# Chunked attention with memory, then a gated feed-forward layer: loads and clears in another order, attention paced per block, six tiles' values computed by tokens, one batch's memory rows copied later

## The chip, the core and the metric

The kernel runs on one core of a Trainium2 chip. The core has a matrix engine (TensorE, "PE" in the profile; its weight loads are "PEld"), VectorE ("DVE"), ScalarE ("ACT"), GpSimd ("POOL") and SyncE ("SP"). Each engine works through its own instructions strictly in the order in which the program puts them, and waits at an instruction until what it needs is there. GpSimd and SyncE also issue DMA transfers. Matrix products go into PSUM, from which VectorE or ScalarE copy them to SBUF. The metric is the device time of one execution in microseconds (us).

## The reference

Four batches, 8 heads, 768 tokens, head size 64. Queries go in chunks of 32; each chunk sees 8 memory keys and the 56 keys from 16 before it to 8 after it. The attention output, heads side by side (3072 x 512), goes through a gated layer.

```python
for c in range(nc):                                  # chunks of 32
    k_full = np.concatenate([mem_k, k[:, :, l_start:r_end]], axis=2)
    v_full = np.concatenate([mem_v, v[:, :, l_start:r_end]], axis=2)
    scores = scale * np.matmul(q_c, k_full.transpose(0, 1, 3, 2))
    a = np.exp(scores - np.max(scores, axis=-1, keepdims=True))
    a = a / (np.sum(a, axis=-1, keepdims=True) + 1e-09)
    out[:, :, c_start:c_end] = np.matmul(a, v_full)
x = out.transpose(0, 2, 1, 3).reshape(B * S, H * D)  # 3072 x 512
gate = np.maximum(x @ w_gate, 0.0)                   # 512 x 1536
val = x @ w_val
result = gate * val @ w_out                          # 1536 x 512
```

## The kernel before

The 3072 tokens are 24 tiles of 128, six to a batch; tile a has four chunks. Tiles are gathered into seven blocks of 3, 3, 4, 4, 4, 4 and 2 tiles (`BLOCKS`), the units of the feed-forward layer.

**Attention of one tile a.** The names are those of the planner's operations, with the line of the work. `t(a,1)` and `t(a,0)` turn keys and queries around: for tiles 0 to 13 on TensorE, for two tiles at once (L221, a "pair": K3 is the load of the keys of tiles 6 and 7), for later ones by a DMA transpose on SP (L261; the keys of tile 14 still on TensorE, L252). `tc` copies them to kT and qT. `s(a)` are the scores (L287, 32 small products), `max`, `sub`, `sum`, `rec`, `nrm` the softmax on VectorE (L300, L307, L319, L323, L330), `exp` on ScalarE (L315). `p(a)` turns the probabilities around: on TensorE up to tile 13 (L336, copied by `pc`), by a DMA transpose from tile 14 on (L340). `v(a)` multiplies them by the values (L353): the stationary operand is a 128 x 128 piece of `v_bd`, in which two heads' memory and context rows stand on the diagonal, and 32 columns of probabilities stream through it, 16 products to a tile. The result has features on the partitions; `x(a)` copies it to `xT`, one buffer to a block, two buffers in all.

**v_bd.** There are two sets, used by batches in turn. Set 0 is filled for batch 0 by four spread copies of a pattern (L171, VectorE), set 1 is cleared by four memsets on GpSimd (L128, "z0" to "z3"). Into them go the values by DMA (L179) and the memory rows, for batches 1 to 3 by eight copies on VectorE each, `mr(b, ...)` (L159). v(6) to v(11) need all of `mr(1, ...)`.

**Feed-forward.** `f(block, m, 0)` and `f(block, m, 1)` are the products with w_gate and w_val for the m-th 128 of the 1536 columns (L378, four matmuls each), then `relu` on ScalarE (L384), `gate` on VectorE (L390). `o(block, tile, ...)` is the product with w_out (L399), copied out by ScalarE (L88) and stored by SP (L409). Blocks 0 and 1 run interleaved, by quarters of the weights (w0 to w3), since the weights arrive in four groups of four DMAs; the later blocks run one after the other.

**Order.** The program is written out by a planner, `schedule()`, which goes through a list of operations with assumed durations, due times and priorities, and gives every engine its order. At run time only the order remains, with the semaphores between engines. Loads go on GpSimd in the order of the string `LOADS`; each DMA of GpSimd waits for the eighth before it to land. `pace(a)` says which first-layer product must have been started before the attention work of tile a may be: `LEAD[block]` products ahead of an even spread. `MEM_LEAD[b]` says how many tiles ahead of batch b's first scores its memory rows may be copied. Early on, where TensorE would sit idle, the plan puts in idle products of 128 x 128 (L370), whose results nobody reads.

Of the kernel before, what the change touches and what calls it, by code (L numbers as in the profile page):

```python
# [20 lines left out]
def kernel(  # L21
# [12 lines left out]
    nc = tc.nc  # L34
# [15 lines left out]
    CTX = 16 + CH + 8  # L50
    NSET = 2
    BLOCKS = [3, 3, 4, 4, 4, 4, 2]
    LEAD = [0, 0, 0, 4, 4, 4, 4, 4]
    LAST = ((0, 384), (384, 512))
    BY_DMA = (14, 15)
    BY_DMA_P = 14
    LANDING = 3.0
    PAIRS = 7
    MEM_BY_SP = 0
    MEM_LEAD = (0, 4, 4, 4)  # L60
    BESIDE = 13.0
    LOADS = """K0 Q0 i K1 Q1 v00 v01 K2 v02 v03 Q2 w0 v10 v11 v12 v13 w1 z0 w2 z1
               K3 z2 w3 z3 m Q3 K4 o0 o1 Q4 K5 b1 Q5 K6 Q6 k14 q14 k15 q15 k16 b2 q16 k17
               q17 k18 q18 k19 q19 k20 q20 k21 q21 k22 b3 q22 k23 q23"""

    KEY_RUNS = ((CH, KW, 0), (0, CH, NMEM), (KW, 64, KW))
    assert sum(BLOCKS) == NT and NMEM == 8 and D == 64 and H == 8

    const = ctx.enter_context(tc.tile_pool(name="const", bufs=1))
    ldpool = ctx.enter_context(tc.tile_pool(name="ldpool", bufs=15))  # L70
    ktpool = ctx.enter_context(tc.tile_pool(name="ktpool", bufs=6))
    prpool = ctx.enter_context(tc.tile_pool(name="prpool", bufs=6))
    kvpool = ctx.enter_context(tc.tile_pool(name="kvpool", bufs=2))
    smpool = ctx.enter_context(tc.tile_pool(name="smpool", bufs=2))
    xtpool = ctx.enter_context(tc.tile_pool(name="xtpool", bufs=2))
    gvpool = ctx.enter_context(tc.tile_pool(name="gvpool", bufs=2))
    grpool = ctx.enter_context(tc.tile_pool(name="grpool", bufs=3))
    opool = ctx.enter_context(tc.tile_pool(name="opool", bufs=3))
# [7 lines left out]
    def copy(eng, o, i):  # L86
        if eng is nc.scalar:
            nc.scalar.copy(o, i)  # L88
        else:
            eng.tensor_copy(o, i)  # L90
# [124 lines left out]
    def pair_t(r, i):  # L215
        ps = TMP["pair", r, i] = aps.tile([128, 2, HP, 128], BF16, tag="aps", name="qk_ps")
        x = qk_b.pop(("pair", r, i))
        for j in range(2):
            for hp in range(HP):
                for r in range(2):  # L220
                    nc.tensor.transpose(ps[D * r:D * r + D, j, hp, :], x[:, 2 * hp + r, j, :], ident_b)  # L221
# [124 lines left out]
    def values(a):  # L346
# [3 lines left out]
        for hp in range(HP):  # L350
            for g in range(4):
                r = slice(CH * g, CH * g + CH)
                nc.tensor.matmul(ps[:, hp, r], lhsT=v_bd[b % NSET][:, hp, 4 * t + g, :],  # L353
                                 rhs=x[:, hp, r], start=True, stop=True)

    def x_copy(a, eng):
        blk = block_of[a]
        j = a - starts[blk]
        if j == 0:
            xTs[blk] = xtpool.tile([128, NFC, 128 * BLOCKS[blk]], F16, name="xT")  # L360
        copy(eng, xTs[blk][:, :, 128 * j:128 * j + 128], TMP.pop(("x", a)))
# [45 lines left out]
    def store(blk, t, cols):  # L407
# [8 lines left out]

    ops, loads = {}, []
    room = {"aps": 2, "sps": 1, "fps": 4, "mx": 2, "dif": 2, "p": 2, "sm": 2, "rinv": 2, "pn": 2, "pT": 6,
            "qk": 15, "xT": 2, "gv": 2, "gr": 3, "o": 3, "kv": 2, "pr": 6, "kt": 6}

    def op(key, eng, fn, deps=(), prio=(0,), take=(), give=(), after=()):
        ops[key] = dict(eng=eng, fn=fn, deps=list(deps), prio=prio, take=list(take), give=list(give),
                        after=list(after))
# [4 lines left out]
    def psum(n):  # L428
        return {"ACT": 0.21 + 0.83e-3 * n, "DVE": 0.22 + 1.04e-3 * n}
# [34 lines left out]
    for a in range(NT):  # L464
        b, t = divmod(a, TPB)
        last = t == TPB - 1
        for i in (1, 0):
            if a < 2 * PAIRS:
                if a % 2:
                    continue  # L470
                op(("t", a, i), {"PE": 0.48}, lambda e, a=a, i=i: pair_t(a // 2, i), [("qk2", a // 2, i), "ib", ("new", b)],
                   (1, a - i, 0), ["aps"], ["pr"], pace(max(a - i, 0)))
                if i:
                    for j in range(2):
                        op(("tc", a + j, i), psum(HP * 128), lambda e, a=a, j=j: pair_k_copy(a // 2, j, engine[e]),
                           [("tc", a, i) if j else ("t", a, i)], (1, a - i, j), (), ["aps"] * j)
# [30 lines left out]
        else:  # L507
# [1 line left out]
            op(("pc", a), {"PE": 0.01}, lambda e: None, [("p", a)], (1, a, 9))  # L509
        blk = block_of[a]  # L510
        j = a - starts[blk]
        op(("v", a), {"PE": 0.45}, lambda e, a=a: values(a),
           [("pc", a)] + [("vl", b, 0 if b else t // 3, n) for n in range(2 if b else 2 * HP)]
           + ([("mr", b, par, hp) for par in range(2) for hp in range(HP)] if b else []), (1, a, 10), ["aps"] + (["xT"] if j == 0 else []), ["pT"],
           [("v", a - 1)] if a else [])
        op(("x", a), psum(HP * 128), lambda e, a=a: x_copy(a, engine[e]), [("v", a)], (1, a, 11), (), ["aps"],
           [("x", a - 1)] if a else [])


    n_early = sum(x < TPB for x in starts)  # L520
# [60 lines left out]
        load(("z", hp), 0, 1.5, lambda: zero(nc.gpsimd, v_bd[1], hp))  # L581

    def load_batch(b):
        deps = [("z", HP - 1)] if b < NSET else [("v", TPB * (b - NSET + 1) - 1)]
        for par in range(2):
            for hp in range(HP):
                if b <= MEM_BY_SP:
                    op(("mr", b, par, hp), {"SP": 0.73}, lambda e, b=b, par=par, hp=hp: mem_rows(b, par, hp, nc.sync),
                       deps + [(("vm", par), 0.2)], (0, par, hp))
                else:  # L590
                    op(("mr", b, par, hp), {"DVE": 0.6}, lambda e, b=b, par=par, hp=hp: mem_rows(b, par, hp, nc.vector),
                       deps + [("vm", par)], (1.5,), (), (), [("s", TPB * b - MEM_LEAD[b])])
        for par in range(2):
            load_v_op(b, 0, par, 0, HP * NCH, par, [], deps)
# [26 lines left out]
    def timed(d):  # L621
        return isinstance(d, tuple) and len(d) == 2 and isinstance(d[1], float)

    MOVE = {"t": 1.3, "p": 1.3, "mr": 0.7}

    def schedule():
        done, started, times = {}, set(), [0.7]
# [28 lines left out]
        while len(started) < len(ops) + len(loads):  # L656
# [8 lines left out]
            while moved:  # L665
                moved = False
                for e in ("POOL", "PE", "ACT", "DVE", "SP"):
# [18 lines left out]
                    else:  # L686
# [15 lines left out]
                        d = o["eng"][e] * (1.8 if e == "PE" and t < 24.0 and key[0] in ("t", "p") else 1.0)  # L702
                        end = t + d
                        done[key] = end + (0.25 if e == "PE" else 0.08)
                        if e == "SP" and key[0] in "tp":
# [55 lines left out]
```

## Time and profile before

| | us |
|---|---|
| median of 3 runs (lowest, highest) | 245.66 (244.87, 248.21) |
| the profiled execution, of which the page tells | 247.63 |
| its span, first to last instruction | 245.9 |
| first feed-forward product starts | 27.53 |
| first w_out product starts | 70.76 |
| VectorE, ScalarE, GpSimd busy | 151.1, 110.6, 76.8 |

The page's slices divide the span in 40 equal parts of 6.1 us. DMAs keep busy up to about 130 us, when the last queries have landed:

```profile
DMA  7999999999999999999994232530112211012102
```

Groups of instructions are told by line, engine and tile, with the number of instructions, busy time, mean duration of one, and the idle time just before them with what ended it. A matmul's own duration includes the fill of the array; what it costs in a row of matmuls is the distance from start to start. In time lines the columns are start, busy time, engine, line, what is done, and in brackets the idle time before. In lists of waits they are the total, the number, and the longest.

### The profile page before, as it was taken

The numbers are of one execution on the slowest core, as the hardware profiler recorded it, in microseconds if no ns is written. First come the engines' busy times: TensorE is split into PE (matmuls) and PEld (weight loads), VectorE is DVE, ScalarE is ACT, GpSimd is POOL, SyncE is SP. The second block draws the span as 40 slices with busy tenths as digits, with TensorE's granted clock in tenths as the row PEclk, the third lists the DMA queues.
The fourth block names the chain that finished last, engine by engine and source line by source line (L and its number), as shares of the span: only waits on it lengthen the run. The fifth ranks groups of instructions, "written<-read, shape, count | busy, mean of one in ns | idle before, by whom it ended". The sixth has DMA issues, their size and how long they took to land.

```text
span 245.9 us, 6041 instructions
## 1 busy us (share of the span) xinstructions
PE 231.0 (94%) x2528; PEld 127.9 (52%) x2528; DVE 151.1 (61%) x270; ACT 110.6 (45%) x232; POOL 76.8 (31%) x88
## 2 busy tenths in 40 slices
PE   0969989969999999999999999999999999999994
PEld 0858656545654644544544444544444444444872
DVE  2886785596889867778937776427871166310430
ACT  2546744434664447645424653235452234312432
POOL 7799999952445554418000000000000000000000
PEclk9997999997999999999999999999999999999999
DMA  7999999999999999999994232530112211012102
GB/s 78 130 125 175 158 198 179 154 199 167 139 138 181 198 174 202 147 151 122 146 195 123 44 67 43 156 104 3 21 24 64 89 43 21 0 40 91 43 4 85
DMA packets 111612, 27.18 MB, mean 111 GB/s; under 512 B 102752, under 2 KB 108640, under 8 KB 111584
## 3 DMA queue, kind: packets, MB, share of 16 engines
q0 software_dynamic: 91840, 16.61, 92.3%
q1 hardware_dynamic: 19744, 10.18, 18.1%
q8 instruction: 20, 0.33, 0.5%
q14 instruction: 8, 0.07, 0.1%
HBM read 33.24 MB, written 6.29 MB: 161 GB/s over the span
## 4 chain that ended last, share of the span: by engine, by line
PE 76%; POOL 10%; DMA 7%; DVE 3%; issue 2%; SPq 1%; ACT 0%; DVEq 0%
PE out_ps L399 26%; PE v_ps L378 22%; PE g_ps L378 22%; POOL v_bd L179 3%; PE xT_ps L353 3%; DMA w_val_sb<-in_moe_w_val_dram 3%; DMA vmem<-in_mem_v_dram 3%; POOL v_bd L128 2%; POOL w_gate_sb L114 2%; PE s_ps L287 2%; POOL w_val_sb L114 2%; DVE v_bd L159 2%; DMA vmem_f<-in_mem_v_dram 1%; PE qk_ps L221 1%; POOL qk_p L210 1%
## 5 line engine op out<-in xcount | busy, mean ns | idle before, releaser
L390 DVE TENSOR_TENSOR gvT<-v_ps,g_relu 128x512 f16<-128x512 f32 (+2 forms) x84 | 51.4, 612 | 55.2 <-PE v_ps L378 42.5
L378 PE MATMUL v_ps<-xT,w_val_sb 128*128 128x512 f16 (+2 forms) x336 | 77.1, 353 | 0.7 <-DMA w_val_sb<-in_moe_w_val_dram 0.7
L378 PE MATMUL g_ps<-xT,w_gate_sb 128*128 128x512 f16 (+2 forms) x336 | 76.7, 352 | 0.3 <-DMA w_gate_sb<-in_moe_w_gate_dram 0.3
L384 ACT ACTIVATE g_relu<-g_ps 128x512 f16<-128x512 f32 (+2 forms) x84 | 44.9, 535 | 55.0 <-PE g_ps L378 49.4
L399 PE MATMUL out_ps<-w_out_sb,gvT 128*128 128x512 f16 (+2 forms) x300 | 65.3, 371 | 0.0
L378 PEld LDWEIGHTS <-w_val_sb 128*128 128x128 f16 x336 | 31.8, 99 | 28.0 <-issue 2.0
L378 PEld LDWEIGHTS <-w_gate_sb 128*128 128x128 f16 x336 | 31.7, 98 | 27.2 <-issue 1.1
L399 PEld LDWEIGHTS <-gvT 128*128 128x128 f16 x300 | 27.9, 98 | 30.4
L179 POOL DMA_DIRECT2D v_bd<-in_v_dram x24 | 27.7, 1165 | 13.1 <-issue 9.1
L88 ACT COPY o_sb<-out_ps 128x512 f32<-128x512 f32 (+2 forms) x25 | 14.2, 566 | 37.6 <-PE out_ps L399 37.5
L315 ACT ACTIVATE p_exp<-dif 128x64 f16<-128x64 f32 (+2 forms) x72 | 19.5, 336 | 9.6 <-DVE dif L307 9.6
L159 DVE COPY v_bd<-vmem 8x1536 f16<-8x1536 f16 x24 | 18.7, 798 | 1.2 <-DMA vmem<-in_mem_v_dram 1.0
L300 DVE TENSOR_REDUCE mx<-s_ps 128x8 f32<-128x512 f32 x24 | 16.6, 690 | 3.5 <-PE s_ps L287 3.1
L319 DVE TENSOR_REDUCE sm<-p_exp 128x8 f32<-128x512 f16 x24 | 16.3, 677 | 3.5 <-ACT p_exp L315 3.1
L330 DVE TENSOR_TENSOR p_n<-p_exp,rinv 128x512 f16<-128x512 f16 x24 | 16.4, 685 | 0.3
L307 DVE TENSOR_TENSOR dif<-s_ps,mx 128x512 f32<-128x512 f32 x24 | 16.4, 682 | 0.2
L353 PEld LDWEIGHTS <-v_bd 128*128 128x128 f16 x384 | 12.7, 96 | 4.7 <-issue 0.3
L88 ACT CAST xT<-xT_ps 128x512 f16<-128x512 f32 x17 | 9.9, 585 | 8.8 <-PE xT_ps L353 8.8
L201 POOL DMA_DIRECT2D qk_b<-in_k_dram x10 | 8.9, 887 | 15.6 <-issue 8.8
L353 PE MATMUL xT_ps<-pT,v_bd 128*128 128x32 f16 x384 | 13.2, 176 | 0.0
L221 PE MATMUL qk_ps<-ident_b,qk_p 128*64 128x128 bf16 x224 | 10.6, 248 | 2.3 <-DMA qk_p<-in_k_dram 2.3
L88 ACT COPY kT<-qk_ps 128x512 bf16<-128x512 bf16 x10 | 7.1, 742 | 12.3 <-PE qk_ps L221 6.3
(46 smaller groups left out, 136.5 us busy)
## 6 DMA issues: line engine op xcount, KB each, us to landing
out_dram<-o_sb SPq DMA_DIRECT2D x23, 256.0 KB, 2.4
v_bd<-in_v_dram POOLq DMA_DIRECT2D x5, 672.0 KB, 16.0
qk_p<-in_k_dram POOLq DMA_DIRECT2D x7, 256.0 KB, 5.7
qk_p<-in_q_dram POOLq DMA_DIRECT2D x7, 256.0 KB, 6.5
w_gate_sb<-in_moe_w_gate_dram POOLq DMA_DIRECT2D x8, 192.0 KB, 5.4
w_val_sb<-in_moe_w_val_dram POOLq DMA_DIRECT2D x8, 192.0 KB, 6.3
w_out_sb<-in_moe_w_out_dram POOLq DMA_DIRECT2D x2, 768.0 KB, 11.4
qk_b<-in_k_dram POOLq DMA_DIRECT2D x10, 128.0 KB, 12.9
```

The lines of the kernel that those rows point to most:

```text
L88: nc.scalar.copy(o, i)
L159: eng.tensor_copy(o, i)
L179: nc.gpsimd.dma_start(dst[64 * par + NMEM + s0:64 * par + NMEM + s1, c0:c1, D * par:D * par + D], bass.AP(tensor=v.tensor, offset=v[b, HP ...
L300: nc.vector.reduce_max(SM[a, "mx"], s4, axis=AX.X)
L307: nc.vector.tensor_tensor(out=SM[a, "dif"].rearrange("p (m r) a s -> p r m a s", r=2), in0=S_ps.pop(a).rearrange("p r (m a) s -> p r m a s ...
L315: nc.scalar.activation(p[:, :, :, s0:s0 + k1 - k0], dif[:, :, :, k0:k1], ACT.Exp, scale=SCALE)
L330: nc.vector.tensor_tensor(out=P_n[a], in0=SM.pop((a, "p")), in1=rinv_b, op=ALU.mult)
L353: nc.tensor.matmul(ps[:, hp, r], lhsT=v_bd[b % NSET][:, hp, 4 * t + g, :], rhs=x[:, hp, r], start=True, stop=True)
L378: nc.tensor.matmul(ps, lhsT=w[:, f, 128 * m:128 * m + 128], rhs=xTs[blk][:, f, :], start=(f == 0), stop=(f == NFC - 1))
L384: nc.scalar.activation(st["r", m], st.pop((0, m)), ACT.Relu)
L390: nc.vector.tensor_tensor(out=st["gv"][:, m, :], in0=st.pop((1, m)), in1=st.pop(("r", m)), op=ALU.mult)
L399: nc.tensor.matmul(st["o", t, cols], lhsT=st["gv"][:, m, 128 * t:128 * t + 128], rhs=w_out_sb[:, m, slice(*cols)], start=(m == 0), stop=(m ...
```

## The change

- `LOADS` is permuted: all pair loads of tiles 0 to 5 and two of the clears stand ahead of the first half of batch 0's values; weight groups w0, w1 and w2 stand ahead of the second half; w3 follows; two clears (z0, z3) and w_out come later, and the single loads of tiles 14 to 23 are no longer in the order of the tiles.
- `LEAD` differs from block to block, so attention is put at other places between the feed-forward products.
- `MEM_LEAD` of batch 1 goes from 4 to 0: its memory rows are copied after the scores of tile 6 in the plan (in the order that results, after those of tile 9) rather than of tile 2.
- For tiles 18 to 23 (`BY_DMA_X`), the values are computed with the probabilities as the stationary operand, 128 rows by 32 columns, and 128 columns of `v_bd` streaming: the result has tokens on the partitions. `xn_copy` brings it to a new buffer and a DMA transpose on SP puts it into `xT`.
- `ldpool` has 14 buffers, not 15, `ktpool` 5, not 6, and there is a new pool of 2 for the copied values.
- Some assumed durations and dependences of the planner differ: a pair's transpose 0.57 for 0.48, a copy of memory rows 0.8 for 0.6, and loads of batch 1 depend on all four clears.

The number of TensorE products in the feed-forward layer, of scores, and of bytes loaded is unchanged. There are 111 idle products, where there were 119.

```diff
-    LEAD = [0, 0, 0, 4, 4, 4, 4, 4]
+    LEAD = [14, 5, -1, 2, 4, 15, 3, 13]
-    MEM_LEAD = (0, 4, 4, 4)
+    BY_DMA_X = 18
+    MEM_LEAD = (0,0,4,4)
-    LOADS = """K0 Q0 i K1 Q1 v00 v01 K2 v02 v03 Q2 w0 v10 v11 v12 v13 w1 z0 w2 z1
-               K3 z2 w3 z3 m Q3 K4 o0 o1 Q4 K5 b1 Q5 K6 Q6 k14 q14 k15 q15 k16 b2 q16 k17
-               q17 k18 q18 k19 q19 k20 q20 k21 q21 k22 b3 q22 k23 q23"""
+    LOADS = """K0 i Q0 Q1 K1 K2 Q2 z2 z1 v00 v03 v01 v02 w0 w1 w2 v12 v11 v13 v10
+               w3 K3 Q3 K4 z0 z3 Q4 k14 K5 k20 o1 m q14 o0 b1 q21 k15 K6 Q5 k21
+               Q6 q15 k23 q19 q16 b2 q18 k17 k18 q20 k16 k22 k19 q17 b3 q23 q22"""
...
-    ldpool = ctx.enter_context(tc.tile_pool(name="ldpool", bufs=15))
-    ktpool = ctx.enter_context(tc.tile_pool(name="ktpool", bufs=6))
+    ldpool = ctx.enter_context(tc.tile_pool(name="ldpool", bufs=14))
+    ktpool = ctx.enter_context(tc.tile_pool(name="ktpool", bufs=5))
+    xnpool = ctx.enter_context(tc.tile_pool(name="xnpool", bufs=2))
...
+    def values_q(a):
+        b, t = divmod(a, TPB)
+        ps = TMP["x", a] = aps.tile([128, HP, 128], F32, tag="aps", name="x_ps")
+        x = PT.pop(a)
+        for hp in range(HP):
+            for g in range(4):
+                r = slice(CH * g, CH * g + CH)
+                nc.tensor.matmul(ps[r, hp, :], lhsT=x[:, hp, r],
+                                 rhs=v_bd[b % NSET][:, hp, 4 * t + g, :], start=True, stop=True)
+    def xn_copy(a, eng):
+        TMP["xn", a] = xnpool.tile([128, HP * 128], F16, name="x_n")
+        copy(eng, TMP["xn", a], TMP.pop(("x", a)).rearrange("p h d -> p (h d)"))
+    def x_dma(a):
+        blk = block_of[a]
+        j = a - starts[blk]
+        if j == 0:
+            xTs[blk] = xtpool.tile([128, NFC, 128 * BLOCKS[blk]], F16, name="xT")
+        nc.sync.dma_start_transpose(xTs[blk][:, :, 128 * j:128 * j + 128], TMP.pop(("xn", a)))
...
-                op(("t", a, i), {"PE": 0.48}, lambda e, a=a, i=i: pair_t(a // 2, i), [("qk2", a // 2, i), "ib", ("new", b)],
+                op(("t", a, i), {"PE": 0.57}, lambda e, a=a, i=i: pair_t(a // 2, i), [("qk2", a // 2, i), "ib", ("new", b)],
...
+        if a < BY_DMA_X:
...
+        else:
+            op(("v", a), {"PE": 0.23}, lambda e, a=a: values_q(a), [("pc", a)] + ready, (1, a, 10),
+               ["aps"], ["pT"], [("v", a - 1)])
+            op(("xc", a), psum(HP * 128), lambda e, a=a: xn_copy(a, engine[e]), [("v", a)], (1, a, 11), ["xn"], ["aps"])
+            op(("x", a), {"SP": 1.3}, lambda e, a=a: x_dma(a), [("xc", a)], (1, a, 12), ["xT"] if j == 0 else [],
+               ["xn"], [("x", a - 1)])
...
-        deps = [("z", HP - 1)] if b < NSET else [("v", TPB * (b - NSET + 1) - 1)]
+        deps = [("z", x) for x in range(HP)] if b < NSET else [("v", TPB * (b - NSET + 1) - 1)]
...
-                    op(("mr", b, par, hp), {"DVE": 0.6}, lambda e, b=b, par=par, hp=hp: mem_rows(b, par, hp, nc.vector),
+                    op(("mr", b, par, hp), {"DVE": 0.8}, lambda e, b=b, par=par, hp=hp: mem_rows(b, par, hp, nc.vector),
```

The orders that the changed program gives its engines, as far as the prediction uses them. TensorE: transposes and scores of the first tiles among idle products, v(0), v(1), v(2), then f(0, 0..8) with s(5), p(3), p(4), p(5) between, v(3) v(4) v(5), f(0,9,0), f(1,0) to f(1,8) with t(6,1) after f(1,2,0), t(6,0), s(6), t(8,1), s(7), t(8,0) between, the rest of blocks 0 and 1, s(9), the w_out products of blocks 0 and 1 with p(8), p(9) between and v(6) to v(9) near their end, then block 2. VectorE: `mr(1, ...)` after nrm(8), then `mr(2, ...)`. SP: the transposes of xT stand among those of the probabilities of tiles 20 to 23 and the stores.

More of the change, by code (lines that the diff above doesn't have):

```diff
@@ L418 @@
     room = {"aps": 2, "sps": 1, "fps": 4, "mx": 2, "dif": 2, "p": 2, "sm": 2, "rinv": 2, "pn": 2, "pT": 6,
-            "qk": 15, "xT": 2, "gv": 2, "gr": 3, "o": 3, "kv": 2, "pr": 6, "kt": 6}
+            "qk": 14, "xT": 2, "gv": 2, "gr": 3, "o": 3, "kv": 2, "pr": 6, "xn": 2, "kt": 5}
     def op(key, eng, fn, deps=(), prio=(0,), take=(), give=(), after=()):
@@ L511 @@
         j = a - starts[blk]
[L512 to L517, printed above, removed]
+        ready = [("vl", b, 0 if b else t // 3, n) for n in range(2 if b else 2 * HP)]
+        ready += [("mr", b, par, hp) for par in range(2) for hp in range(HP)] if b else []
+        if a < BY_DMA_X:
+            op(("v", a), {"PE": 0.45}, lambda e, a=a: values(a), [("pc", a)] + ready, (1, a, 10),
+               ["aps"] + (["xT"] if j == 0 else []), ["pT"], [("v", a - 1)] if a else [])
+            op(("x", a), psum(HP * 128), lambda e, a=a: x_copy(a, engine[e]), [("v", a)], (1, a, 11), (), ["aps"],
+               [("x", a - 1)] if a else [])
+        else:
[4 more added lines that the diff above has]
+               ["xn"], [("x", a - 1)])
     n_early = sum(x < TPB for x in starts)
@@ L622, in timed @@
         return isinstance(d, tuple) and len(d) == 2 and isinstance(d[1], float)
-    MOVE = {"t": 1.3, "p": 1.3, "mr": 0.7}
+    MOVE = {"t": 1.3, "p": 1.3, "x": 1.3, "mr": 0.7}
     def schedule():
@@ L704, in schedule @@
                         done[key] = end + (0.25 if e == "PE" else 0.08)
-                        if e == "SP" and key[0] in "tp":
+                        if e == "SP" and key[0] in "tpx":
                             done[key] = end + (BESIDE if n_load < len(loads) or t < done["qk", NT - 1, 0] else LANDING)
```

## The prediction

> **What bounds the kernel now.** First the page's busy line and clock row, then busy time by stretch of the span.
>
> ```profile
> PE 231.0 (94%) x2528; PEld 127.9 (52%) x2528; DVE 151.1 (61%) x270; ACT 110.6 (45%) x232; POOL 76.8 (31%) x88
> ...
> PEclk9997999997999999999999999999999999999999
> ```
> ```profile
> 26.00:40.00 14.00, 12.79 (x175) 8.46 (x173) 10.84 (x23) 7.39 (x18) 13.82 (x18) 1.00 1.62 181
> 40.00:55.00 15.00, 12.99 (x146) 7.68 (x145) 11.10 (x16) 5.92 (x10) 12.44 (x12) 1.00 1.34 176
> 55.00:66.00 11.00, 11.00 (x100) 6.04 (x98) 7.71 (x16) 5.44 (x14) 2.28 (x3) 0.84 2.10 158
> ```
> (Columns: stretch, length, busy PE, PEld, DVE, ACT, POOL; granted clock; DMA share; GB/s.) From 55 us on TensorE is busy in all of every stretch up to its last product, at full clock but for 3.4 us (the 0.84 here, the 7 in the tenth slice). So time can come from three places only: when the first product of the second layer starts, TensorE's idle and half-clock time after that, and how much TensorE work there is. Its waits, longest first:
>
> ```profile
> PE s_ps L287 <- DVE kT L90: 2.0, 1, 2.0
> ...
> PE v_ps L378 <- DMA w_val_sb<-in_moe_w_val_dram: 0.7, 1, 0.7
> ...
> PE g_ps L378 <- DMA w_gate_sb<-in_moe_w_gate_dram: 0.3, 1, 0.3
> ```
> The 2.0 us are explained by VectorE and GpSimd in order of time:
>
> ```profile
> 47.97 2.13 DVE L159 COPY v_bd<-vmem 8x1536 f16<-8x1536 f16 x1
> ...
> 50.49 2.11 DVE L159 COPY v_bd<-vmem 8x1536 f16<-8x1536 f16 x1
> ...
> 53.92 0.70 DVE L90 COPY kT<-qk_ps 128x512 bf16<-128x512 bf16 x1
> ```
> ```profile
> 47.53 2.22 POOL L179 DMA_DIRECT2D v_bd<-in_v_dram  x1 [0.41 <-issue]
> 50.05 2.19 POOL L179 DMA_DIRECT2D v_bd<-in_v_dram  x1 [0.30 <-issue]
> ```
> Two of batch 1's memory-row copies take 2.1 us in place of 0.54, each ending just after a 2.2 us issue by GpSimd. Behind them in VectorE's order stands the key copy (53.92) for which the scores wait. The four products after the gap (55.64 to 59.18) take 1.28, 1.28, 0.98 and 0.73 us where 0.65 is normal. The granted clock was 0.5 there, from 55.45 to 58.86: 1.65 us lost.
>
> The start, on ScalarE, then TensorE:
>
> ```profile
> 19.06 0.73 ACT L88 COPY kT<-qk_ps 128x512 bf16<-128x512 bf16 x1 [3.20 <-PE qk_ps L221]
> 19.70 0.58 ACT L88 COPY pT<-pT_ps 128x512 f16<-128x512 f16 x1
> 20.18 0.81 ACT L315 ACTIVATE p_exp<-dif 128x64 f16<-128x64 f32 x3
> ```
> ```profile
> 27.53 0.82 PE L378 MATMUL g_ps<-xT,w_gate_sb 128*128 128x384 f16 x4
> ```
> Tile 2's exponential, ready since 18.3, stands behind a copy of K2, whose load landed only at 17.91; the first product waits for tile 2's values.
>
> **The change, part by part.**
>
> *Start.* GpSimd issues a pair load in 0.90, a v piece in 0.78, a weight piece in 0.62, a clear in 1.35; a pair load's transfer takes 1.5 at this point (landing events of the trace at 5.90, 7.38, 8.84, 10.30). In the new order all six pair loads and two clears come before v. GpSimd's idle 2.46 (5.5 to 7.9) is filled by K2, Q2 and part of the clears. K2 then lands at 11.8 and Q2 at 13.3; the nine v pieces are issued from 10.0 to 17.2, and the last lands at about 20.0 (2.8 after issue); w0 is issued 17.2 to 19.7 and lands by 24.0 (25.89 before). K1 moves back 1.5 (10.3). Following tiles 0 to 2 by row durations in the new orders of TensorE, VectorE and ScalarE: scores 0 at 10.9, scores 1 at 13.5 (13.1 before), scores 2 at 16.0, values 0 at 20.1 (v's landing), values 2 at 23.9, the first product at 25.1. That is 2.4 earlier. But the two clears now run beside VectorE's four spread copies (6.69 to 10.49). One of those took 1.20 in place of 0.95 beside a short issue. If each excludes the other, 2.8 of clears delay the fourth spread to 13.3, scores 1 by 2.0, and the first product to 27.1. Ends 0.4 and 2.4; I take the middle, 1.4 earlier (26.1), since the rows show both a mild and a full block.
>
> *Weights before v's second half.* In the new TensorE order the first product is followed by all of block 0's products for w0, w1, w2 (18 of 0.65 = 11.7, and 1.0 of scores and transposes). A weight piece takes 1.0 of transfer, so a group lands every 4.0 and feeds 3.9: by 28, 32 and w3 by 40.6. The waits of 0.72 and 0.33 go (1.05). Then comes a tight place: values 3 to 5 need v's second half, whose eight pieces now wait for slots behind w1 and w2 (each of GpSimd's DMAs waits for the eighth before it) and land at 36.6, where TensorE arrives at 37.8 to 38.8; the product of w3 is needed 1.2 later and its gate half lands at 38.6; K3 lands at 42.0 to 43.5, needed at 43.2 to 44.2. Three slacks of about one microsecond, each with an uncertainty as large: I charge +0.7 in all (0 to 2.5).
>
> *Batch 1's memory rows later.* The eight copies now stand after scores 9. What was behind them (key copies, gates) is free: the gap of 2.0 and the half clock of 1.65 go. Next late there would be the key load K4, which lands at 45.3 and is needed at about 49. The copies (8 x 0.80 by their mean, 6.4) now run beside the second layer's output products, where VectorE has no gates: from about 67 to 75. Their reader, values 6, comes at 78. The vmem load behind the first half of w_out lands at about 54, batch 1's v (after the whole of w_out) at 70 to 72 (72.20 before).
>
> *Values by tokens, tiles 18 to 23.* Rows by shape, count | busy, mean:
>
> ```profile
> L353 PE MATMUL xT_ps<-pT,v_bd 128*128 128x32 f16 x384 | 13.2, 176 | 0.0
> L221 PE MATMUL qk_ps<-ident_b,qk_p 128*64 128x128 bf16 x224 | 10.6, 248 | 2.3 <-DMA qk_p<-in_k_dram 2.3
> ...
> L287 PE MATMUL s_ps<-kT,qT 64*32 64x64 bf16 x704 | 7.7, 194 | 3.6 <-DVE kT L90 2.0 <-DVE dif L307 1.1 <-ACT qT L88 0.5
> ```
> Start to start, 16 of the first take 0.40; 16 of the second 0.57 (full rows, 64 columns); 32 of the third 0.25. The new form (full rows, 32 columns, 128 streamed) is not in the trace: 16 products cost 0.57 at worst if they overlap no better than the 64-column row, 0.21 if four run side by side (a quarter of 16 x 0.054). I take 0.31, nearer the 32-column row that overlaps well: 6 x -0.09 = -0.5 (-1.1 to +1.0). Their transposes go on SP (1.2 of issue, 2.5 to land); p of tiles 20 to 23 and the stores queue behind them, with 4 us of slack (p 20 before its values) and 10 us (block 6's products), so nothing. The scores already change the shape in use, and a product ahead of them is 0.09 longer; with such a loss at each tile the term would be 0. The Trainium skill ("TensorEngine Tiling (Array Packing)", Key Properties) says as a rule that changing the tiling mode drains TensorE; by that rule, and these 0.09, the sum would be -5.4.
>
> *The rest.* Pacing, two clears past w3 and K3, and smaller load and key pools move work within a stretch where TensorE never waits; POOL's late loads (K16 after the transpose of tile 14) land at about 103 for scores at 118: nothing.
>
> **Sum.** -1.4 -1.05 -2.0 -1.65 -0.5 +0.7 = -5.9. The profiled execution took 247.63 (span 245.9), 1.97 over the median of 245.66. Against its own time: 241.7. Against the median the same sum gives 239.8. The runs of 244.87 to 248.21 spread by about a half-clock window, so part of the 1.65 may be missing in the median's run. I take the middle, 240.7.
>
> **Rivals.**
> 1. *The clears shut out the spreads altogether* (0.24). First product at 27.1, sum -4.9: 242.7 or 240.8, so 241.7. For: the 2.1 us copies. Against: three spreads that overlapped three issues with 0.25 lost. The Trainium skill ("SBUF — State Buffer", Who interferes with whom) states that rule: the second to issue blocks fully until the first ends.
> 2. *The memory-row copies are blocked again at the new place* (0.16). Batch 2's two 2.2 us issues fall at about 74 to 78; if three of the copies for batch 1 meet them or their neighbours, values 6 come 2 late and a half-clock window follows: 240.7 + 3.6 = 244.3.
> 3. *Slower: v's second half starves TensorE* (0.10). After 18 products there is nothing to run but values 3. Each microsecond that v lands after 38.8 is one of idle, and 1.65 more once a window goes to half clock. At 43 all the gain is gone; at 48, after a pile-up of v's issues behind slots, it is 250.7. Against: before, v pieces landed 0.6 apart.
>
> **Chances.** Forecast 0.50. Two per cent (4.9 us, about what this kernel's runs can tell) puts the bound at 240.75, in the middle of the forecast's spread. Faster: 0.50 x 0.75 (its own range, 237.5 to 242.5, leans low if the start gives all 2.4) + 0.24 x 0.35 + 0.16 x 0.1 = 0.47. Slower: 0.07 of rival 3 and a little of rival 2: 0.08. Within: 0.45. Range: all terms at their good ends against the median, 237, to rival 2 with a late start, 246.
>
> **What would show it.** First product near 26.1 (25.1 to 27.1); no wait on VectorE's key copy and no half clock between 50 and 60; the first output product at 64 to 65 (70.76 before); memory-row copies of batch 1 done before values 6; 16 products of the new values in under 0.40. A TensorE wait of over 1 us before values 3, the first w3 product, or values 6 would make me wrong.

## The result, and the profile after

The changed kernel takes 244.34 us (median of 20 runs, 243.56 to 244.88). The kernel before, run beside it, took 246.14 (20 runs, 244.36 to 248.34). Medians and ranges in this document take all executions, ratios and intervals only those within 1.5% of the fastest of the same kernel. The ratio is 0.9929, with a 95% interval from 0.991 to 0.9948: 0.7% faster, where 240.7, some 2%, was forecast. The profiled execution of after took 244.88 (span 243.1), 2.75 less than that of before; the prediction's sum was -5.9.

The page's clock row of after, then busy time by stretch (length, busy PE, PEld, DVE, ACT, POOL; granted clock; DMA share; GB/s):

```profile
PEclk9997999999999999999999999999999999999999
```
```profile
26.00:40.00 14.00, 12.95 (x145) 8.33 (x143) 10.66 (x22) 7.38 (x19) 9.47 (x14) 1.00 1.56 169
40.00:55.00 15.00, 14.35 (x195) 8.94 (x192) 7.11 (x13) 7.39 (x15) 14.62 (x17) 1.00 1.64 170
```

The half-clock window at 55 is gone, and so is the gap at 52: TensorE is busy 14.35 of the second stretch, where it was 12.99. Of 26 to 40 almost nothing has been won (12.95 for 12.79). TensorE's two longest waits in after behind the first load (total, number, longest):

```profile
PE s_ps L289 <- DVE dif L309: 2.2, 1, 2.2
PE v_ps L401 <- PE g_ps L401: 0.8, 1, 0.8
```

The key copy and w_val are no longer in the list; waits of 0.3 on w_gate and on a copy of xT remain. New are the 2.2, a wait of tile 1's scores for VectorE at 16 us, and 0.8 ahead of the second value product, put down to TensorE itself. The first product of the feed-forward layer:

```profile
28.12 0.81 PE L401 MATMUL g_ps<-xT,w_gate_sb 128*128 128x384 f16 x4
```

28.12 stands where 27.53 stood, and where 26.1 was forecast. Cut at the first product, the first w_out product and the last one, the span shows where time went. The last column is the same kernel with its two early clears put elsewhere, the first experiment below.

| us of the profiled execution | before | after | forecast change | after, clears behind w2 |
|---|---|---|---|---|
| start to first FFN product | 27.53 | 28.12 | -1.4 | 25.84 |
| from there to first w_out product | 43.23 | 40.60 | -4.0 | 40.05 |
| from there to last w_out product | 171.63 | 171.27 | -0.5 | 171.27 |
| rest of the span | 3.47 | 3.12 | 0 | 3.11 |

The start lost 0.6 instead of gaining 1.4. VectorE's and GpSimd's rows at the start of after tell why:

```profile
4.47 2.00 DVE L464 CAST kmem_b<-kmem_f 128x128 bf16<-128x128 f32 x1 [1.42 <-DMA kmem_f<-in_mem_k_dram]
7.15 2.95 DVE L242 COPY kT<-kmemT 128x768 bf16<-128x768 bf16 x1 [0.68 <-ACT kmemT L467]
...
10.47 3.81 DVE L173 COPY v_bd<-vmem 128x3072 f16<-128x3072 f16 x4
...
14.56 0.69 DVE L302 TENSOR_REDUCE mx<-s_ps 128x8 f32<-128x512 f32 x1
```
```profile
7.13 2.75 POOL L130 MEMSET v_bd<- 128x1536 f32 x2
11.72 7.52 POOL L181 DMA_DIRECT2D v_bd<-in_v_dram  x9 [1.84 <-DVE v_bd L173]
```

The copy of batch 0's memory keys into kT took 0.36 before and takes 2.95 here. It starts 0.02 after the first of two back-to-back clears and ends 0.22 after the second. The four spreads stand behind it in VectorE's order and start at 10.47 (6.69 before). Behind the spreads stand tile 0's maxima (14.56; 11.63 before), though TensorE had its scores ready at 11.6, and on GpSimd v's first issue waits 1.84 for the first spread. So the attention of tiles 0 to 2 and all loads from v on came late: w0 landed at 28.18, where I had placed it at 24.0, v's second half at 41.92 (36.6), w3's gate half at 44.10 (38.6), K3 at 47.76 (42.0 to 43.5).

### The profile page after: what moved, and what is told of

Same layout as the page of the kernel before. It is cut to its first block, busy times and chain, and to the rows that moved or that the text cites. A ratio compares the mean times of both kernels' runs of the same rounds, so it can differ in the third digit from the quotient of the medians.

```text
span 243.1 us, 6043 instructions
## 1 busy us (share of the span) xinstructions
PE 228.8 (94%) x2520; PEld 125.1 (51%) x2520; DVE 149.3 (61%) x264; ACT 113.7 (47%) x238; POOL 77.8 (32%) x88
## 4 chain that ended last, share of the span: by engine, by line
PE 81%; DMA 10%; POOL 4%; issue 2%; DVE 1%; SPq 0%; ACT 0%; DVEq 0%
PE out_ps L422 26%; PE v_ps L401 24%; PE g_ps L401 24%; DMA w_val_sb<-in_moe_w_val_dram 6%; POOL v_bd L181 4%; DMA w_gate_sb<-in_moe_w_gate_dram 2%; PE xT_ps L355 2%; PE qk_ps L223 2%; PE s_ps L289 2%; DMA kmem_f<-in_mem_k_dram 1%; PE x_ps L365 1%; DVE kmem_b L464 1%; POOL w_gate_sb L116 1%; PE pT_ps L338 1%; DVE v_bd L173 0%
## 5 line engine op out<-in xcount | busy, mean ns | idle before, releaser
L401 PE MATMUL v_ps<-xT,w_val_sb 128*128 128x512 f16 (+2 forms) x336 | 76.0, 349 | 0.8 <-PE g_ps L401 0.8
L401 PE MATMUL g_ps<-xT,w_gate_sb 128*128 128x512 f16 (+2 forms) x336 | 75.9, 349 | 0.4 <-DMA w_gate_sb<-in_moe_w_gate_dram 0.3
L401 PEld LDWEIGHTS <-w_val_sb 128*128 128x128 f16 x336 | 31.0, 98 | 27.3 <-issue 1.2
L161 DVE COPY v_bd<-vmem 8x1536 f16<-8x1536 f16 x24 | 15.7, 686 | 0.2
L203 POOL DMA_DIRECT2D qk_b<-in_q_dram x10 | 9.4, 943 | 13.4 <-DMA qT<-qk_b 7.4
L355 PEld LDWEIGHTS <-v_bd 128*128 128x128 f16 x288 | 9.3, 96 | 3.7 <-issue 1.4
L393 PE MATMUL idle_ps<-ident_h 128*128 128x128 f16 x111 | 10.5, 250 | 0.0
L289 PE MATMUL s_ps<-kT,qT 64*32 64x64 bf16 (+2 forms) x768 | 7.8, 194 | 2.6 <-DVE dif L309 2.2
L355 PE MATMUL xT_ps<-pT,v_bd 128*128 128x32 f16 x288 | 9.6, 176 | 0.7 <-ACT xT L90 0.3
L223 PE MATMUL qk_ps<-ident_b,qk_p 128*64 128x128 bf16 x224 | 9.9, 237 | 0.3 <-DMA qk_p<-in_q_dram 0.2
```

Source lines behind the costliest of these rows:

```text
L401: nc.tensor.matmul(ps, lhsT=w[:, f, 128 * m:128 * m + 128], rhs=xTs[blk][:, f, :], start=(f == 0), stop=(f == NFC - 1))
```

## The experiments

The experiments ran in three sets, each with the kernel before beside it, the first on another chip than the two later ones. Before took 245.92 beside "two clears behind w2", "two clears early in before", "rows later" and "no values by tokens"; 245.22 beside "weights ahead", "v's second half first", "old pacing" and "tokens from tile 15"; and 245.56 beside "one clear", "key memory on ScalarE" and "more idle products". Across sets, the ratio to before is the safer measure.

In the first, the third and the last experiment below, the edit leaves the orders of TensorE, VectorE, ScalarE and SyncE as they were; in the others the planner also wrote another order for some engines.

### The two early clears, moved and added

```diff
-    ... K1 K2 Q2 z2 z1 v00 v03 v01 v02 w0 w1 w2 v12 ...
+    ... K1 K2 Q2 v00 v03 v01 v02 w0 w1 w2 z2 z1 v12 ...
```

The orders of TensorE, VectorE, ScalarE and SyncE stay as in after.

> The changed kernel with the two early clears (z2, z1) moved from ahead of batch 0's values to behind weight group w2; the orders of TensorE, VectorE, ScalarE and SP are the same to the last instruction. Theory (the clears shut VectorE's copies out): the batch 0 copy of memory keys takes 0.4 us again in place of 2.95, the fourth spread ends by 11 (14.27 now), the first product starts at 25 to 26 (28.12 now), the time falls by 1.5 to 2.5 us to about 242.3. Rival (the new order of the pair loads, K1 behind Q1, is what makes the start late): the first product stays within 0.5 of 28.1 and the time within 0.5 of 244.3.

Measured: 241.88 (four runs, 241.54 to 242.33), ratio to before 0.9848 [0.9823, 0.9873], 2.46 under after; by the ratios, 0.9929 and 0.9848, it is 2.0. VectorE, then TensorE:

```profile
5.29 0.36 DVE L242 COPY kT<-kmemT 128x768 bf16<-128x768 bf16 x1 [0.68 <-ACT kmemT L467]
...
6.81 4.04 DVE L173 COPY v_bd<-vmem 128x3072 f16<-128x3072 f16 x4
...
12.34 0.69 DVE L302 TENSOR_REDUCE mx<-s_ps 128x8 f32<-128x512 f32 x1
```
```profile
25.84 0.81 PE L401 MATMUL g_ps<-xT,w_gate_sb 128*128 128x384 f16 x4
```

The copy is short again, the maxima come 2.22 earlier than in after and the first product 2.28 earlier. The landings are near those that I had placed: w0 24.32, v's second half 37.14, w3's gate half 39.83, K3 43.70. Nothing else in the program moved, so the two clears at that place cost 2.0 to 2.5, and the rival, the order of the pair loads, is out.

Other profiles agree: the first product comes at 28.33 in the other version with both clears early (no values by tokens), and at 25.05, 25.23 and 26.31 in three others with the clears behind w2 (tokens from tile 15, more idle products, old pacing). After's profile also has half clock from 17.7 to 21.1, which this one has not; but five of after's 20 runs show a full clock, and they lie at 243.76 to 244.35, still some 2 above 241.88. One part stays unexplained: the cast of kmem_f (the memory keys, brought to bf16 ahead of their transpose), VectorE's first link of this chain, ends at 4.62 here and at 6.47 in after, where the first clear starts only at 7.13 (taken up at the end).

The other way around, the same two clears are put early into the kernel before:

```diff
-    LOADS = """K0 Q0 i K1 Q1 v00 v01 ... v13 w1 z0 w2 z1
-               K3 z2 w3 z3 m ...
+    LOADS = """K0 Q0 i K1 Q1 z2 z1 v00 v01 ... v13 w1 z0 w2
+               K3 w3 z3 m ...
```

> The kernel before, with only z2 and z1 moved into GpSimd's idle 2.46 us ahead of batch 0's first values. Theory (shut out): the copy of memory keys takes about 2.9 in place of 0.36, the spreads end near 13, the first product starts 1 to 2.5 later than 27.5, the time is 0.5 to 2 us above the kernel before. Rival (they fill idle time and cost nothing, and free GpSimd later): the first product within 0.5 of 27.5, the time equal or up to 1 us lower.

Measured: 249.26 (six runs, 248.53 to 250.33), ratio 1.0156 [1.0127, 1.0186], 3.3 slower: the direction as expected, the size above it. GpSimd fills with the clears the time in which it would have waited, and still VectorE pays:

```profile
3.75 4.45 DVE L440 CAST ident_b<-ident_h 128x128 bf16<-128x128 f16 x1 [2.32 <-POOL ident_h masks.py:199]
4.34 3.92 DVE L441 CAST kmem_b<-kmem_f 128x128 bf16<-128x128 f32 x1
...
9.68 3.81 DVE L171 COPY v_bd<-vmem 128x3072 f16<-128x3072 f16 x4
```
```profile
5.43 2.72 POOL L128 MEMSET v_bd<- 128x1536 f32 x2
```

Here the victims are others, the two casts ahead of the first transpose: 4.45 for 0.20 and 3.92 for 0.59, to 0.05 and 0.12 after the clears' end. They were held from 3.75 on, 1.7 before the first clear, beside two pair-load issues (3.68 to 5.44) that the clears follow without a gap; in before the same two issues end at 5.48, and the casts were through by 4.62.

Tile 0's maxima come 2.60 later than in before and the first product, at 29.11, 1.58 later. That is about half of the 3.3. The rest is not the clears' alone: TensorE's order differs from its 229th product on, it waits 1.62 for tile probabilities at 36.1, and half clock follows from 37.7 to 41.1; all six runs show a clock of 0.991 to 0.993.

### One clear instead of two

```diff
-    ... K2 Q2 z2 z1 v00 v03 v01 v02 w0 w1 w2 v12 ...
+    ... K2 Q2 z2 v00 v03 v01 v02 w0 w1 w2 z1 v12 ...
```

> The changed kernel with one of its two early clears (z1) moved behind w2, the other (z2) left ahead of v; the orders of TensorE, VectorE, ScalarE and SyncE are the same. Theory (VectorE's copy of the memory keys into kT waits until GpSimd's clears are done, and the spreads, tile 0's maxima and v's first issue follow it): that copy ends just after the end of the one clear, 1.4 earlier than with two, the first product at 26.4 to 27.1 (28.12 with two, 25.84 with none), time 242.5 to 243.3. Rival (any clear ahead of v costs the same, or the cast beside the pair-load issues is what counts): first product at 27.6 or more, 243.8 or more.

Measured: 241.9 (four runs, 241.45 to 242.08), ratio 0.9838 [0.9767, 0.9909], first product at 26.01: as good as with no clear there. Both expectations missed.

```profile
6.17 0.36 DVE L242 COPY kT<-kmemT 128x768 bf16<-128x768 bf16 x1 [0.68 <-ACT kmemT L467]
...
6.90 5.31 DVE L173 COPY v_bd<-vmem 128x3072 f16<-128x3072 f16 x4
```
```profile
7.34 2.08 POOL L130 MEMSET v_bd<- 128x1536 f32 x1
```

The key copy was through before the clear began, because the cast ahead of it took 1.37 here and not 2.00, so the clear met the spreads: 5.31 for the four, 1.3 more than without it, and 2.08 for the clear, which alone takes 1.4. Tile 0's maxima start at 12.49, only 0.15 later, because VectorE stood idle 1.28 ahead of them when there is no clear. The cost of a clear is not proportional: here the first 1.3 us have cover, and a second clear would have none.

### The key memory on ScalarE, both clears left early

```diff
-    op("kmb", {"DVE": 0.25}, lambda e: nc.vector.tensor_copy(kmem_b, kmem_f), [("kml", 1.5)], prio=(-6,),
-       after=["ib"])
+    op("kmb", {"ACT": 0.35}, lambda e: nc.scalar.copy(kmem_b, kmem_f), [("kml", 1.5)], prio=(-6,),
+       after=["warm2"])
...
-        nc.vector.tensor_copy(
+        copy(nc.vector if b else nc.scalar,
```

> The changed kernel with both clears left early, and with the cast of kmem_f and batch 0's copy of the memory keys into kT on ScalarE in place of VectorE. Theory A (only that VectorE copy and the cast were stretched, the clears do not hinder the spreads, as the forecast's good end had it): the spreads run from about 6.8 to 11 and the first product comes at 25.5 to 26.2, time 241.5 to 242.5. Theory B (the clears stretch whatever VectorE copies within SBUF beside them, so the first spread takes the place of the victim, the first rival of the prediction): a spread of 2 us or more ends with the second clear at about 10, the fourth at about 12.9, the first product at 26.6 to 27.4, time 242.6 to 243.8. Rival C (ScalarE's copies are stretched by the clears too): first product at 27.8 or later.

Measured: 243.63 (nine runs at 242.99 to 245.41, one at 300.7), ratio 0.9925 [0.9887, 0.9964], first product at 27.76. VectorE, then GpSimd:

```profile
6.84 6.57 DVE L173 COPY v_bd<-vmem 128x3072 f16<-128x3072 f16 x4
...
13.70 0.69 DVE L302 TENSOR_REDUCE mx<-s_ps 128x8 f32<-128x512 f32 x1
```
```profile
7.28 4.21 POOL L130 MEMSET v_bd<- 128x1536 f32 x2
```

ScalarE's cast and copy take 0.30 and 0.83 and are through at 5.94, before the clears; so this run says nothing of such ScalarE work beside a clear. ScalarE's copies of keys and queries out of PSUM do run beside the clears, from 7.21 and 9.59, and take 1.34 and 1.31, where they take 1.36 and 1.32 with the clears behind w2: rival C is out for those. The spreads take the place of the victim, as theory B has it: one by one they last 1.20, 2.21, 2.21 and 1.19, and the clears 2.08 and 2.18, each waiting for the other in turn. The fourth spread ends at 13.42 (theory B said 12.9) and the maxima come 1.36 later than without early clears. The first product is 0.36 past theory B's end: on top of the 1.36, TensorE waited 0.52 within the values of tile 0 for the last of v's nine pieces, which landed at 22.90, 2.24 after the one ahead of it. Why that piece was late is open. The good end of my first term, where clears do not hinder spreads, falls.

### Batch 1's memory rows

```diff
-    MEM_LEAD = (0, 4, 4, 4)
+    MEM_LEAD = (0, 0, 4, 4)
```

> The kernel before, with only batch 1's memory rows copied later (MEM_LEAD of batch 1 from 4 to 0). Theory (this alone carries the gain): the 2.0 us wait on the key copy near 52 is gone and with it the half clock behind it; the profile gains 2.0 to 3.7, the median 1.5 to 2.5 us (to about 244.2), and the spread of the runs shrinks to 1.5 us. Rival (the copies are blocked again at the new place, or another wait takes over): a new wait of over 1 us between 60 and 90, the median within 0.5 of the kernel before.

This is the kernel before with nothing else changed. Its profiled execution took 244.59, 3.04 less than that of before: no gap at 52, and no half clock before the last product. But its runs fall in two groups, five at 244.2 to 245.0 and six at 247.3 to 249.4, with one more at 337.4. The median of all twelve is 247.43, 1.5 above before, where 244.2 was expected; the ratio, of the runs that count for it, is 0.9984 [0.9946, 1.0021]. What the rows are worth in a median is not measured by it. The upper group shows a clock of 0.993, one half-clock window; a window of 3.4 us costs 1.7, so it makes up about half of the distance between the groups. The waits of the profiled run suggest where it could come from, since TensorE stands 2.2 us between 31 and 36:

```profile
PE v_ps L378 <- DMA w_val_sb<-in_moe_w_val_dram: 1.2, 1, 1.2
...
PE g_ps L378 <- DMA w_gate_sb<-in_moe_w_gate_dram: 1.0, 1, 1.0
```

To test that, w0, w1 and w2 also go ahead of v's second half, in the kernel before:

```diff
-    MEM_LEAD = (0, 4, 4, 4)
+    MEM_LEAD = (0, 0, 4, 4)
-    LOADS = """... Q2 w0 v10 v11 v12 v13 w1 z0 w2 z1
+    LOADS = """... Q2 w0 w1 w2 v10 v11 v12 v13 z0 z1
```

> The kernel before with batch 1's memory rows later (as in the run that was 244.2 to 245.0 or 247.3 to 249.4), and with w0, w1, w2 ahead of v's second half. Theory A (the slow half of those runs came from a half-clock window that the waits for w1 at 31 to 34 bring on): no weight waits before 35, all runs together within 1.5 us, at 243 to 244.5. Rival (the unsteadiness has another source): two groups of runs, 2 to 3 us apart, again.

Measured: 244.33, ratio 0.9968 [0.9935, 1.0002]. No wait on weights is left, and ten of twelve runs lie at 243.9 to 244.8; one of 245.24 and one of 247.15 remain. The upper group has shrunk from six of eleven to one or two of twelve, not vanished as theory A would have it. That the waits for weights bring the window on is likely, and not shown: the planner's order of TensorE's products changed with the loads, too.

In the changed kernel MEM_LEAD is not what holds the rows back. With 4 in place of 0 there (clears behind w2), the planner writes the very same program: in its plan the rows wait for z0 and z3, which now stand behind K4.

### The weights' order, the pacing, the values by tokens

All but the last start from the changed kernel with its clears behind w2 (241.88). First, v's second half again ahead of w1 and w2:

```diff
-    ... v02 w0 w1 w2 z2 z1 v12 v11 v13 v10
+    ... v02 w0 v12 v11 v13 v10 w1 w2 z2 z1
```

> The changed kernel with its two early clears behind w2 (241.88 in the first set), and with v's second half again ahead of w1 and w2. Theory A (the new weights order removes real TensorE waits, about as much as the profile of before shows on weights, 1.05, up to the 2.2 of the run with the rows later): waits on w_gate and w_val of 1 to 2.2 us together between 27 and 36 come back, the 0.9 wait ahead of the second value product may go, and the time is 242.3 to 244, some runs 1.6 more where a half-clock window follows. Rival (the tight places behind the new order, values 3 to 5 and w3, cost as much as the weight waits): 241.4 to 242.2.

Measured: 241.95 (241.57 to 244.45), ratio 0.9874 [0.9821, 0.9926]. The time is the rival's, but its reason is not shown. No wait on weights came back in the profile, and there is no tight place either: with this order of loads the planner puts the values of tiles 3, 4 and 5 between the products of block 0 and 1, at 33.1, 36.1 and 39.3. The profiled run is the slowest of the six; a wait of 1.43 within tile 1's values, at matmul 349 and of the kind treated below, was followed by half clock from 26.4 to 29.8.

Then the old pacing:

```diff
-    LEAD = [14, 5, -1, 2, 4, 15, 3, 13]
+    LEAD = [0, 0, 0, 4, 4, 4, 4, 4]
```

> The changed kernel with its two early clears behind w2, and with LEAD as before (0, 0, 0, 4, 4, 4, 4, 4). Theory (pacing moves work inside a stretch in which TensorE never waits): 241.5 to 242.2, the same as 241.88. Rival (pacing is what keeps TensorE without a wait from block 2 on): a TensorE wait or gap of 1 us or more after 60 and 243 or more.

Measured: 241.69 (240.55 to 242.43), ratio 0.984 [0.9793, 0.9886]. Pacing is worth nothing that these runs resolve. It moves work: the stretch up to the first w_out product is 39.25 here (40.05 with the new pacing), the one to the last is 171.84 (171.27).

Then the values by tokens from tile 15 on:

```diff
-    BY_DMA_X = 18
+    BY_DMA_X = 15
```

> The changed kernel with its two early clears behind w2, and with the values by tokens for tiles 15 to 23 instead of 18 to 23. Theory (0.06 of TensorE time for each tile, SP has room): three tiles more, 0.2 less than 241.88, so 241.5 to 241.9. Rival (SP's queue of transposes becomes late for blocks 3 and 4): waits of TensorE on xT around 115 to 140 and 242.5 or more.

Measured: 247.57 (246.14 to 248.85), ratio 1.009 [1.0057, 1.0122]: 5.7 slower than with 18. TensorE, in time:

```profile
156.21 0.32 PE L289 MATMUL s_ps<-kT,qT 64*32 64x64 bf16 x32 [1.57 <-DVE dif L309]
157.14 0.62 PE L365 MATMUL x_ps<-v_bd,pT 128*32 128x128 f16 x16 [0.62 <-DMA pT<-p_n]
158.99 1.87 PE L401 MATMUL g_ps<-xT,w_gate_sb 128*128 128x512 f16 x4 [1.23 <-DMA xT<-x_n]
```

Three waits within 6 us, 3.4 together, two of them on DMA transposes issued by SP, and half clock from 156.6 to 163.4, which costs as much again. The rival holds, though I had looked for it at 115 to 140. With values by tokens from tile 18 on, TensorE has no such wait.

Last, the changed kernel (clears early) with no values by tokens:

```diff
-    BY_DMA_X = 18
+    BY_DMA_X = 24
```

> The changed kernel with the values of tiles 18 to 23 as in the kernel before (BY_DMA_X 24). Theory: 6 tiles x 0.06 us more of TensorE (0.40 against 0.34 for a tile), so 0.4 above the changed kernel, about 244.7. Rival (the six transposes on SP and a change of the array's mode cost as much as they save): the time equal to the changed kernel or lower.

Measured: 244.37 (244.0 to 244.95), ratio 0.9946 [0.9927, 0.9966], where after has 244.34 and 0.9929. The 0.4 cannot be told from nothing. The profile speaks for the rival: from the first w_out product to the last it is 171.00 here and 171.27 in after. TensorE's rows at these tiles, shown further down, say why.

### The wait with no cause in the profile

In after TensorE stands 0.83 before f(0,1,1), and 0.89 with the clears moved; its inputs had long been there.

```diff
     for _, fn in schedule():
         fn()
+        if fn is idle_product:
+            n_idle += 1
+            for _ in range({30: 14, 56: 6}.get(n_idle, 0)):
+                fn()
```

(Clears behind w2 here, too.)

> The changed kernel with its two clears behind w2, and with 20 more idle products between 15 and 20 us, where TensorE waited 0.86 and 0.43. The question is the 0.4 to 0.9 us for which TensorE stood before f(0,1,1), its matmul 476, with nothing that the profile shows to wait for. Theory (TensorE waits for its next block of instructions, 16 KB to a fetch): the wait stays at matmul 476, which is now the 24th product of s(5), 1.2 to 1.7 after the end of a fetch on the instruction queue. Rival (it belongs to the product f(0,1,1), its PSUM buffer or its inputs): it stays before f(0,1,1), now matmul 496. The time, 241.5 to 243, decides nothing.

Measured: 241.99 (a single run), and the wait stays at matmul 476, now within the scores of tile 5:

```profile
25.97 0.27 PE L289 MATMUL s_ps<-kT,qT 64*32 64x64 bf16 x24
27.67 0.22 PE L289 MATMUL s_ps<-kT,qT 64*32 64x64 bf16 x8 [1.42 <-issue]
```

The 24 scores in front of it are those that the theory counted. A packet of 16 KB on the instruction queue ended at 26.33, 1.34 earlier. A second such wait came up at matmul 349 (0.41, 1.47 after another packet). So the wait belongs to the place in the instruction stream, not to the product. In six other profiled runs of the changed kernel it stands at 476 (0.41 to 0.89), 1.3 to 1.6 after a packet's end; in the version of before with the weights ahead, at 475 (0.85). That it is a wait for instructions is inferred from the place and the packets: the profile names no such cause, and packets also end where TensorE does not wait. The Trainium skill ("Runtime: NRT & Kernel Launch", Instruction fetch mechanics) says that instructions are refilled in blocks of 16 KiB, 256 instructions, and that the cost of crossing a block's boundary is mostly hidden. The first fits: 349 and 476 are 127 matmuls apart, 254 instructions with their weight loads. If these waits are the refills, the second does not hold here, where they cost up to 1.43.

## Why the prediction was wrong, point by point

- **Start: -1.4, measured +0.59. This is the step that failed.** Its first half was right: without the clears the load order brings the first product to 25.84 (25.05 to 26.31 in four profiles), 1.7 earlier than before, where the good end had 2.4. The failure is in the price of the clears, for which I took half a block on the spreads and a full block, 27.1, as the worst. I had looked at the spreads alone, and not at VectorE's cast and key copy, which stand ahead of them and, with the pair loads issued back to back, run beside GpSimd too. The clears cost 2.28 of the first product instead of 1.0, and the full price, 28.12, lies past what I took as the worst. This term makes up 2.0 of the 3.15 by which the profiled executions miss the sum. Then I let the loads run by GpSimd's own durations, although v's first issue waits for a spread, so that a VectorE copy held up shifts the landings as well.
- **Weight waits -1.05, tight places +0.7.** The waits went, as forecast. The tight places took about 1.0 (0.27 and 0.33, and the slower products around them at 42 to 44), at landings 4 to 6 us later than placed, and the 0.83 at matmul 476 came, which I had not foreseen. In the changed kernel the old order of v and w1 costs nothing measurable against the new, so this part is worth nothing in the end.
- **Memory rows -2.0 and -1.65.** Both are gone from the profile, and the copies, mostly 0.50 to 0.95, were done before the values of tile 6. But the median had less of it to give. The profiled execution of before lies 1.5 above its 20 runs' median; that of after 0.5 above. So 2.75 between the profiled executions are 1.80 between the medians. I had met this by going half way, to 240.7. My remark that the first runs spread by about a half-clock window was off: they spread by 3.3, and a window costs 1.7.
- **Values by tokens -0.5, measured about +0.2.** From the first of the 16 products to the next product behind them the new form takes 0.34 in place of 0.40, near the 0.31 that I took. But I left out what lies ahead of them. The new form in after, then the old form at the same tile in the run with no values by tokens:

```profile
161.43 1.04 PE L401 MATMUL v_ps<-xT,w_val_sb 128*128 128x512 f16 x4
162.40 0.41 PE L365 MATMUL x_ps<-v_bd,pT 128*32 128x128 f16 x16
162.74 1.04 PE L401 MATMUL g_ps<-xT,w_gate_sb 128*128 128x512 f16 x4
```
```profile
160.61 1.04 PE L401 MATMUL v_ps<-xT,w_val_sb 128*128 128x512 f16 x4
161.48 0.56 PE L355 MATMUL xT_ps<-pT,v_bd 128*128 128x32 f16 x16
161.88 1.02 PE L401 MATMUL g_ps<-xT,w_gate_sb 128*128 128x512 f16 x4
```

  The four products ahead take 0.97 up to the new form and 0.87 up to the old one. From the last product ahead to the first behind, a tile takes 0.65 with the new form, at all six tiles, and 0.62 with the old: 0.03 more, not 0.06 to 0.09 less. Within the new form four products do start within 0.01 of each other, and the next four some 0.05 later, so four run side by side. The loss is at the ends, 0.09 ahead of the first and about 0.1 behind the last. The prediction had named such a loss at each tile, with the term at 0, and left it out of its sum.
- **The rest at nothing.** Pacing: right for the time. The 0.36 between the first and the last w_out product is not the new form's; with the old pacing it is not there (171.84), and the stretch ahead is shorter instead. The 0.35 behind the last w_out product were not forecast, and I have no reason for them.
- **The rivals.** Rival 1 had the mechanism, a full block, with the victim one step too late and the price too small. The Trainium skill ("SBUF — State Buffer", Who interferes with whom) says that, in VectorE's two-port modes, the one of VectorE and GpSimd that issues second blocks fully; spreads and clears that alternate at 2.21 and 2.08 agree. It does not tell why the key copy, waiting since 7.15, was not let in when the first clear ended at 8.57. Rival 2 did not happen: one copy of 2.20, for batch 2, harmed nothing. Rival 3 did not happen: values 3 started 0.14 after v's landing, with no wait over 0.33.

With the clears moved the kernel takes 241.88, and the 241.7 of the prediction's own sum lies near. That is partly luck. The span of its profile is 5.6 shorter than that of before, for the 5.9 of the sum, with start and rows about as placed; but the sum was counted from an execution 1.5 above the median, and between medians the change is 4.0. It is 1.5% faster than before and 0.8 to 1.0% faster than after, the best of this study together with the one-clear, the old-pacing and the v-first versions, from which it cannot be told apart.

What stays open is the cast of kmem_f. It lasts 2.00 in after, and 2.35 and 1.37 in two other profiled runs with an early clear, though it ended before the first clear began; it lasted 0.23 to 0.29 in most runs without one, and 0.70 and 0.59 in two. In each of the six profiles where VectorE's cast lasts over 0.5 it ends 0.02 to 0.17 after one of GpSimd's issues or clears does, which fits a cast that is held by GpSimd's unbroken row and let in between two of its instructions. Between which two is open: beside the same issues, casts that started at 4.12 and 4.13 ended at 5.49 and 6.48. It matters, since with a short cast the key copy is through before the first clear (5.65 with the clears behind w2). The clears would then have met the spreads, as they did with the key memory on ScalarE, and tile 0's maxima would have come about 1.4 late and not 2.2.

## What to carry to other kernels

Idle time of GpSimd is not free for work on SBUF: before putting a clear there, list every VectorE copy within SBUF that runs at that moment, from the first link of the chain on, and count the whole clear as lost to it, less the idle time that VectorE has further on. Follow a delayed engine into the queues of those that wait for it; here the loads were late because VectorE was. Price a new form of product from the last product ahead of it to the first behind it, not from its own first to its own last. And before crediting a gap or a half-clock window seen in one profile, look at how the kernel's runs spread: they may not all have it.

## What the runs showed of the hardware that was not expected

- A VectorE copy that started beside two back-to-back clears waited for both (2.95 for 0.36). Two casts that started beside pair-load issues were held through two issues and two clears in a row (4.45 for 0.20, 3.92 for 0.59). A stream of copies and a stream of clears alternate instead (2.21 and 2.08).
- TensorE stood 0.4 to 1.4 us at a fixed place of its instruction stream: in seven profiled runs of the changed kernel at matmul 476, in two at 349. When 20 more products were put ahead, the wait stayed at its number and moved to another product.
- 16 products with a 128 x 32 stationary operand and 128 columns streaming: four start within 0.01 us of each other, the next four some 0.05 later. The change of shape costs 0.09 ahead, so that a tile takes 0.65 between its neighbours, against 0.62 for 16 products of 128 x 128 with 32 columns streaming.
